# Three weight tiles leave SP's queue for GpSimd's, and zero fills change engine

## The chip, the cores and the metric

One core of a Trainium2 chip runs the whole program. The metric is the device time in microseconds of one execution. Engines are named as in the profile: PE (TensorE), DVE (VectorE), ACT (ScalarE), POOL (GpSimd) and SP (SyncE, which here only issues DMAs).

## The reference

A delta-rule recurrence feeds a gated feed-forward block. For 4 batches and 8 heads, 768 tokens of 48 numbers each:

```python
k_n = k / (np.linalg.norm(k, axis=-1, keepdims=True) + 1e-06)
for t in range(S):
    y[:, :, t] = einsum('bhd,bhde->bhe', q[:, :, t], state)
    v_old = einsum('bhde,bhd->bhe', state, kt)
    state = state + bt * einsum('bhd,bhe->bhde', kt, vt - v_old)
x = y.transpose(0, 2, 1, 3).reshape(B * S, H * D)      # 3072 tokens x 384
xn = x / sqrt(mean(x * x, axis=-1) + 1e-06) * rms_g
g = xn @ w_gate                                        # 384 x 1536
out = (g * sigmoid(g) * (xn @ w_val)) @ w_out          # 1536 x 384
```

q, k, v and beta are float32. The three weight matrices arrive as float64 words, which the kernel takes in as 64-bit integers and turns into float32 itself.

## The kernel before, in words

**Chunks.** The 768 tokens are cut into 6 chunks of 128. In a chunk the recurrence becomes matrix products, if one has the inverse of a triangular matrix for each head. For the first chunk `invert_halves` builds the inverses of 16-blocks on DVE in 15 steps (lines L498 and L505), with all 32 batch-heads on the partitions. The result `ttb` must then be turned so that tokens lie on the partitions: it goes out to DRAM as `td` (L507) and comes back as `tt` (L524); a second matrix, made from it by L510, goes out as `nd` (L516, issued by ACT) and comes back as `ne` (also L524). `halves` then multiplies with `tt` (p_vh, L652; its result is copied out by ACT at L659) and with `ne` (p_wh, L663).

**Order.** For the first 60 units of a hand-made plan nothing is scheduled automatically (`tc.manual_schedule()`): each engine, and each engine's DMA queue, executes in the order in which the Python code emits. `begin` emits the norms of k, the key scores (K phase), the query scores (the loop over `n` after `clear_ttb`, here called the Q phase), and the inversion; then `recur(0, ...)` emits the recurrence of the first chunk, up to its first `yield`. The rest is interleaved by `run_plan`, which takes generators by their times. A DMA issued by SP waits at the head of SP's queue until its semaphore's former user has landed and until its buffer is free; all that is behind it waits too.

**Weights.** They come as 18 tiles of 768 KB, each in two loads of 384 KB, in the order of the list `todo`. `fetch` issues the next tile. Tiles 3 to 6 land in parts of the final weight buffers that are still unused (`spare`), the others in a pool of three (`raw`). The generator `weights` turns a tile into float32 in five DVE steps (L259, L268, L280, L284, L290) after one ACT step (`shrink`, L249, the upper words, buffer `top`); `convert(n)` takes n of these DVE steps. At tile 5 and from tile 7 on, a tile's fourth step also calls `fetch`. A tile index below `AHEAD`, which is 9, goes to SP's queue, the others to POOL's.

**Fills.** `stay_warm(n)` emits n matmuls (two PE instructions each in the trace, L190) whose result nobody reads.

**First norms.** `norm` in the first chunk has ACT square and sum y (L871), POOL add 1e-6 (L879) and raise to the power -0.5 (L880, giving `rs`); `scale` and `transpose_y` then give the input `xt` of the feed-forward block (L894), whose matmuls are L923 and L910, with silu by ACT (L932) and the product h_f by DVE (L934).

Of the kernel before, what the change touches and what calls it, by code (L numbers as in the profile page):

```python
# [18 lines left out]
C = 128  # L19
HC = 64  # L20
# [8 lines left out]
def kernel(  # L29
# [21 lines left out]
    nc = tc.nc  # L51
# [4 lines left out]
    DM = H * D  # L56
# [35 lines left out]
    state = [const.tile([128, NP, 2 * D], FP32, name=f"state{b}") for b in range(B)]  # L92
# [16 lines left out]
    lo, hi = slice(0, HC), slice(HC, C)  # L109
# [28 lines left out]
    def setup():  # L138
        for t in kpad + qpad:
            nc.vector.memset(t[:, :, D:DP], 0.0)  # L140
        nc.scalar.memzero(tt_all)
        for n in range(B):
            load_k(n)
        fetch()

        beta_sb = ttb.rearrange("p k j -> p (k j)")[0:BH, 0:S]
        nc.sync.dma_start(out=beta_sb, in_=beta.rearrange("b h s -> (b h) s"))
        blocks = beta.rearrange("b h (c a i) -> a (b h) c i", a=NBLK, i=W)
        for a in range(NBLK):
            nc.sync.dma_start(out=nbeta[a * BH : (a + 1) * BH], in_=blocks[a])  # L150
        load_q(0)
        fetch()
        load_q(1)
        fetch()
        nc.sync.dma_start(out=g_sb, in_=moe_rms_g.rearrange("(t p) -> p t", p=128))
        nc.vector.memset(half, 0.5)
        nc.vector.memset(mhalf, -0.5)
        make_identity(nc, ident)
        row, col = (
            gblk.bitcast(I32).rearrange("p k j -> p (k j)")[:, C * i : C * (i + 1)] for i in (0, 1)  # L160
        )
        nc.gpsimd.iota(row, pattern=[[0, 128]], base=0, channel_multiplier=1)
        nc.gpsimd.iota(col, pattern=[[1, 128]], base=0, channel_multiplier=0)
        nc.vector.memset(mask[lo, 1], 1.0)
        for i, p in enumerate((lo, hi)):
            nc.vector.tensor_tensor(
                out=mask[p, i], in0=row[p, p], in1=col[p, p], op=ALU.is_lt
            )
        p_fill.append(psum.tile([128, DM], FP32, name="p_fill", tag="out", bufs=2))
# [18 lines left out]
    def stay_warm(n, data=wide):  # L188
        for i in range(n):
            nc.tensor.matmul(  # L190
                p_fill[0].rearrange("p (t m) -> p t m", m=128)[:, 0 : data.shape[1]],
                ident,
                data,
                skip_group_check=True,
            )
# [27 lines left out]
    spare = [wgv_sb[:, t : t + 2, far] for t in range(0, 2 * KT, 2)] + [  # L223
        wo_sb[:, FT // 2 : FT // 2 + 4].rearrange("p (x t) m -> p x (t m)", x=2)
    ]
    AHEAD = 3 + len(spare) + 2

    def fetch():
        i = len(raws)
        if i < len(todo):  # L230
            if 3 <= i < 3 + len(spare):
                raw = spare[i - 3].bitcast(I64)
            else:
                raw = bits.tile([128, 2, WT], I64, name="raw", bufs=3)
            for x, src in enumerate(todo[i][1]):
                (nc.sync if i < AHEAD else nc.gpsimd).dma_start(out=raw[:, x], in_=src)
            raws.append(raw)

    def words(raw):
# [14 lines left out]
    def weights():  # L254
        for i, ((dst, src), raw) in enumerate(zip(todo, raws)):
            low, high = words(raw)
            top = tops[i]
            top_u, dst_u = top.bitcast(U32), dst.bitcast(U32)
            nc.vector.tensor_scalar(  # L259
                out=top_u,  # L260
                in0=top_u,
                scalar1=3,
                scalar2=0x7FFFFFFF,
                op0=ALU.logical_shift_left,
                op1=ALU.bitwise_and,
            )
            yield
            nc.vector.scalar_tensor_tensor(  # L268
                out=top_u,
                in0=high,  # L270
                scalar=0x80000000,
                in1=top_u,
                op0=ALU.bitwise_and,
                op1=ALU.bitwise_or,
            )
            yield
            if i + 1 < len(todo):
                tops.append(shrink(raws[i + 1]))

            nc.vector.tensor_scalar(  # L280
                out=dst_u, in0=top_u, scalar1=0xFF800000, scalar2=None, op0=ALU.bitwise_and
            )
            yield
            nc.vector.scalar_tensor_tensor(  # L284
                out=dst, in0=low, scalar=2.0**-52, in1=dst, op0=ALU.mult, op1=ALU.mult
            )
            if i == 5 or i >= 7:
                fetch()
            yield
            nc.vector.tensor_tensor(out=dst, in0=dst, in1=top, op=ALU.add)  # L290
            yield
        bits_pool.close()
# [3 lines left out]
    def convert(steps):  # L296
        for i in range(steps):
            next(conversion, None)
# [174 lines left out]
    def clear_ttb():  # L473
        nc.gpsimd.memset(ttb, 0.0)  # L474
        nc.gpsimd.memset(ttb.rearrange("p j i -> p (j i)")[:, 0 : W * W : W + 1], 1.0)
# [109 lines left out]
    def recur(c, dt):  # L585
# [196 lines left out]
        if c == 0:  # L782

            halved = [halves(b) for b in units]
            next(halved[0])
            next(halved[1])
            next(halved[0])
            next(halved[1])
            corner(0, None)
            corner(1, None)  # L790
            convert(1)
            corner(None, 0)
            corner(None, 1)
            convert(2)
            inner(0, None, 0)
            inner(1, None, 1)
            stay_warm(1)
            inner(None, 0, None)
            inner(None, 1, None)
            convert(1)  # L800
            u_0, u_1 = us[0], us[1]
            stay_warm(2)
            outer(None, 0)
            outer(None, 1)
            convert(3)
            stay_warm(3)
            transpose_y(0, scale(*ys.pop(0)))
            convert(1)
            stay_warm(2)
            transpose_y(1, scale(*ys.pop(1)))  # L810
            convert(4)
            yield
            update(0, u_0)
            mask_queries(2)
            yield dt
            update(1, u_1)
            reload()
            yield dt
            next(halved[2])
            mask_queries(3)  # L820
            yield dt
            next(halved[3])
            yield dt
            next(halved[2])
            yield dt
            corner(2, None)
            next(halved[3])
            yield dt
            corner(3, 2)
            yield dt  # L830
            inner(None, None, 2)
            corner(None, 3)
            yield dt
            inner(2, None, 3)
            yield dt
            inner(3, 2, None)
            yield dt
            u_2, u_3 = us[2], us[3]
            outer(None, 2)
            yield dt  # L840
            inner(None, 3, None)
            yield dt
            outer(None, 3)
            yield dt
            transpose_y(2, scale(*ys.pop(2)))
            yield dt
            transpose_y(3, scale(*ys.pop(3)))
            yield dt
            update(2, u_2)
            yield dt  # L850
            update(3, u_3)
            reload()
            return
# [117 lines left out]

    def begin():
        setup()
        stay_warm(14, ident[:, None])
        norms = [normalize(n) for n in range(B)]
        for n in (0, 0, 1, 1, 2, 2, 3, 0):
            next(norms[n])
        transpose(0, kpad[0], K0)
        tops.append(shrink(raws[0]))
        for n in (3, 1):  # L980
            next(norms[n])
        transpose(1, kpad[1], K0)
        for n in range(B):
            p_gs = score_part(n, K0)
            if n + 2 < B:
                next(norms[n + 2])
                transpose(n + 2, kpad[n + 2], K0)
            keep_keys(n, p_gs)
            convert((1, 2, 2, 5)[n])
        setup_beta()  # L990
        clear_ttb()
        convert(2)
        for n in range(B):
            transpose(n, qpad[n % 2], Q0)
            stay_warm(2)
            load_q(n + 2)
            fetch()
            load_v(n)
            keep_queries(n, score_part(n, Q0))
            if n in (1, 2):  # L1000
                fetch()
            if n == 0:
                mask_queries(n)
        nc.scalar.memzero(gp_all[HC:C, :, 0:HC])
        invert_halves()
        load_k(B)
        stay_warm(4)
        for t in state:
            nc.scalar.memzero(t)
        stay_warm(6, ttb_all[:, 0:DM].rearrange("p (t m) -> p t m", m=128))  # L1010
        convert(3)
        mask_queries(1)
        convert(3)


    CYC = 3 * FT * B // 2
# [49 lines left out]
```

## Time and profile before

| | |
|---|---|
| median of 10 runs | 873.8 us (872.0 to 879.15) |
| the profiled execution | 873.14 us, span 871.4 us |
| PE busy | 826.3 us, 95% of the span |
| DVE busy | 403.0 us, 46% |
| ACT busy | 257.1 us, 30% |
| POOL busy | 98.4 us, 11% |
| DVE busy in 80 to 100 us | 18.84 of 20 us |
| PE's granted clock, 48 to 70 us | 0.50 |

The span is the profiled execution's; about 1.7 us of its time lie around it. Times in a row of the timeline or the chain are counted from the span's start. A row of the timeline has start, duration (first start to last end where rows are merged), engine and line, operation, output <- inputs, form and count. "SPq" and "ACTq" are the queues that issue DMAs; the duration there is that of issuing, and the time to landing is told in the list of DMA issues.

### The profile page before, as it was taken

The page shows a single profiled execution, that of the slowest core. Times are in us where ns is not written, and L with a number is a line of the kernel's source. Part 1 is how long each engine was busy: PE and PEld are TensorE (multiplying, and loading weights), DVE is VectorE, ACT ScalarE, POOL GpSimd, SP SyncE. Part 2 cuts the span into 40 slices and gives each one's busy share as a digit, 9 for nine tenths or more (in the row PEclk, how much of TensorE's full clock was granted, in tenths as well). Part 3 has the DMA queues.
Part 4 walks back from the last instruction along what each step waited for, and adds up shares of the span by engine and source line. Part 5 has one row for each costly group of instructions (what it writes and reads, how often), then busy time and mean ns, then how long its engine had stood idle before and what let it go on. Part 6 is the DMA issues. An engine that isn't in the chain of part 4 may idle for free.

```text
span 871.4 us, 20949 instructions
## 1 busy us (share of the span) xinstructions
PE 826.3 (95%) x8990; PEld 636.7 (73%) x8990; DVE 403.0 (46%) x1014; ACT 257.1 (30%) x663; POOL 98.4 (11%) x130
## 2 busy tenths in 40 slices
PE   7839979798999999999999999999999999999998
PEld 6437767576887777787777787777787777777776
DVE  6826976994343671333671333581333581220100
ACT  5423545312334212334112334112334212220111
POOL 3001244200140000230000140000130000000000
PEclk8958998999999999999999999999999999999999
DMA  7961444303222122122122122122121112000000
GB/s 184 264 170 40 110 128 102 111 1 99 52 66 37 31 76 38 39 65 37 31 76 38 39 65 37 31 72 41 39 51 22 32 70 35 3 19 1 19 0 19
DMA packets 153405, 52.16 MB, mean 60 GB/s; under 512 B 144448, under 2 KB 147520, under 8 KB 153312
## 3 DMA queue, kind: packets, MB, share of 16 engines
q1 hardware_dynamic: 125744, 40.06, 18.6%
q0 software_dynamic: 1440, 7.08, 2.4%
q10 hardware_dynamic: 26128, 3.68, 2.4%
q8 instruction: 71, 1.16, 0.5%
q14 instruction: 22, 0.18, 0.1%
HBM read 36.64 MB, written 14.16 MB: 58 GB/s over the span
## 4 chain that ended last, share of the span: by engine, by line
PE 79%; DVE 13%; issue 2%; ACT 2%; DMA 2%; POOL 1%; SPq 0%; ACTq 0%; DVEq 0%
PE p_gv L923 38%; PE p_o L910 18%; DVE tmp L537 4%; DVE ttb L546 3%; PE p_g L353 3%; PE p_y L688 3%; PE p_z L744 2%; PE p_t L337 2%; PE p_k L726 2%; PE p_y L726 2%; PE p_v L602 2%; PE p_x L762 1%; PE p_z L753 1%; PE p_w L609 1%; DVE h_f L934 1%
## 5 line engine op out<-in xcount | busy, mean ns | idle before, releaser
L923 PE MATMUL p_gv<-xt,wgv_sb 128*128 128x256 f32 x1728 | 413.0, 385 | 0.6 <-DVE xt L894 0.6
L923 PEld LDWEIGHTS p_gv<-xt,wgv_sb 128*128 128x128 f32 x1728 | 320.3, 190 | 63.8 <-issue 3.1
L910 PE MATMUL p_o<-wo_sb,h_f 128*128 128x384 f32 x576 | 215.4, 498 | 11.3 <-DVE h_f L934 11.3
L934 DVE TENSOR_TENSOR h_f<-sil,p_gv 128x256 f32<-128x256 f32 x144 | 60.2, 418 | 242.1 <-ACT sil L932 242.0
L932 ACT ACTIVATE sil<-p_gv 128x256 f32<-128x256 f32 x144 | 55.3, 384 | 333.4 <-PE p_gv L923 316.6
L910 PEld LDWEIGHTS p_o<-wo_sb,h_f 128*128 128x128 f32 x576 | 104.4, 191 | 63.6 <-DVE h_f L934 17.0
L537 DVE SCALAR_TENSOR_TENSOR tmp<-gblk,nbeta,ttb 128x31 f32<-128x31 f32 (+15 forms) x155 | 62.2, 401 | 4.6
L367 DVE TENSOR_TENSOR gp<-p_g,mask 64x128 f32<-64x128 f32 (+1 forms) x160 | 38.0, 277 | 40.0 <-ACT gp L363 35.4
L546 DVE TENSOR_TENSOR ttb<-ttb,tmp 128x31 f32<-128x31 f32 (+15 forms) x155 | 53.0, 342 | 4.9
L317 POOL TENSOR_TENSOR knrm<-ksum,half 128x8 f32<-128x8 f32 x24 | 41.8, 1745 | 66.1 <-DVE ksum L316 66.1
L879 POOL TENSOR_SCALAR ms<-ms 128x1 f32<-128x1 f32 x24 | 6.2, 257 | 322.5 <-ACT y L871 322.0
L342 ACT COPY kqt<-p_t 128x512 f32<-128x512 f32 x48 | 28.1, 585 | 32.4 <-PE p_t L337 31.7
L474 POOL MEMSET ttb<- 128x1024 f32 x6 | 5.7, 955 | 241.5 <-DMA td<-ttb 232.0
L353 PE MATMUL p_g<-kqt 64*64 64x192 f32 x640 | 31.8, 331 | 1.1 <-ACT gp L363 0.9
L744 PEld LDWEIGHTS p_z<-v_raw,tt 64*64 64x64 f32 x768 | 25.8, 142 | 9.2 <-issue 7.2
L622 ACT COPY vs<-p_v 32x256 f32<-32x256 f32 x48 | 17.4, 363 | 44.6 <-PE p_w L609 22.1
L353 PEld LDWEIGHTS p_g<-kqt 64*64 64x64 f32 x640 | 23.3, 132 | 8.4 <-issue 5.3
L762 PE MATMUL p_x<-tt,gp 64*64 64x64 f32 x384 | 28.8, 229 | 0.1
L744 PE MATMUL p_z<-v_raw,tt 64*64 64x48 f32 x768 | 28.8, 227 | 0.0
L362 ACT COPY gp<-p_g 128x128 f32<-128x128 f32 x80 | 21.3, 266 | 20.4 <-PE p_g L353 19.0
L753 PE MATMUL p_z<-u,x 64*64 64x48 f32 x384 | 27.1, 220 | 0.0
L762 PEld LDWEIGHTS p_x<-tt,gp 64*64 64x64 f32 x384 | 25.6, 142 | 1.9 <-issue 1.3
(110 smaller groups left out, 782.7 us busy)
## 6 DMA issues: line engine op xcount, KB each, us to landing
kpad<-in_k_dram SPq DMA_DIRECT2D x24, 192.0 KB, 2.7
qpad<-in_q_dram SPq DMA_DIRECT2D x24, 192.0 KB, 2.6
v_raw<-in_v_dram SPq DMA_DIRECT2D x24, 192.0 KB, 3.0
out_dram<-o_sb SPq DMA_DIRECT2D x24, 192.0 KB, 1.9
gblk<-gd SPq DMA_DIRECT2D x6, 512.0 KB, 3.2
td<-ttb SPq DMA_DIRECT2D x6, 512.0 KB, 2.6
gd<-gp ACTq DMA_DIRECT2D x80, 32.0 KB, 1.7
nd<-gblk SPq DMA_DIRECT2D x5, 512.0 KB, 2.7
```

What stands on the lines that cost most here:

```text
L317: nc.gpsimd.tensor_tensor(out=knrm, in0=ksum, in1=half, op=ALU.pow)
L353: nc.tensor.matmul(to, pair[d, K1 if i else K0], pair[d, places], skip_group_check=True)
L367: nc.vector.tensor_tensor(out=to[p, :, place], in0=p_g[p, :, place], in1=mask[p, i, None].to_broadcast([p.stop, 2, HC]), op=ALU.mult,)
L537: nc.vector.scalar_tensor_tensor(out=tmp, in0=gblk[:, i, None, i + 1 :].to_broadcast(shape), scalar=nbeta[:, c, i : i + 1], in1=ttb[:, 0 : ...
L546: nc.vector.tensor_tensor(out=to, in0=to, in1=tmp, op=ALU.add)
L744: nc.tensor.matmul(p_zs[b_z][p, h], tt[b_z][p, h], r[p, h], start=(h == 0), stop=(p is lo), skip_group_check=True,)
L753: nc.tensor.matmul(p_zs[b_u][hi, h], x2s[b_u][:, h], us[b_u][lo, h], start=False, stop=True, skip_group_check=True,)
L762: nc.tensor.matmul(p_x[lo, h], gp[b_x][hi, h, HC * K0 : HC * (K0 + 1)], tt[b_x][hi, h], skip_group_check=True,)
L910: nc.tensor.matmul(p_o[i], h_f[:, i * C : (i + 1) * C], wo_sb[:, f], start=(f == f0), stop=(f == f1 - 1),)
L923: nc.tensor.matmul(p_gv[:, i], wgv_sb[:, i * KT + t, f * 128 : (f + 1) * 128], xt[:, t], start=(t == 0), stop=(t == KT - 1),)
L932: nc.scalar.activation(out=sil, in_=p_gv[:, 0], func=ACTF.Silu)
L934: nc.vector.tensor_tensor(out=h_f, in0=sil, in1=p_gv[:, 1], op=ALU.mult)
```

## The change

In the Q phase, SP keeps one weight tile in each of the first three passes (tiles 3, 4 and 5). Tiles 6, 7 and 8 are issued on POOL's queue, right after `outer(None, 1)` of the first recurrence, so behind the two first norms' POOL instructions. `fetch` gets the issuing function as an argument in place of the comparison with `AHEAD`. The loads of v for n = 2 and 3 move behind `invert_halves`. The zero fills of the four `state` tiles and of the part of `gp` move from ACT to POOL, to a place ahead of the Q phase. The ACT step for tile 3 (`shrink(raws[3])`) is emitted ahead of `invert_halves`, and `weights` skips it later. Fills: two more behind the inversion, one fewer at each of two places in the recurrence. One conversion step fewer is taken at the end of `begin`. In the changed file, line numbers from `fetch` on are smaller by 1 up to `recur`'s first chunk.

```diff
-        fetch()
+        fetch(nc.sync.dma_start)          # three times, in setup
...
-    AHEAD = 3 + len(spare) + 2
-
-    def fetch():
+
+    def fetch(dma):
         i = len(raws)
...
-                (nc.sync if i < AHEAD else nc.gpsimd).dma_start(out=raw[:, x], in_=src)
+                dma(out=raw[:, x], in_=src)
...
-            if i + 1 < len(todo):
+            if len(tops) == i + 1 < len(todo):
                 tops.append(shrink(raws[i + 1]))
...
             if i == 5 or i >= 7:
-                fetch()
+                fetch(nc.gpsimd.dma_start)
...
             inner(1, None, 1)
-            stay_warm(1)
             inner(None, 0, None)
             inner(None, 1, None)
             convert(1)
             u_0, u_1 = us[0], us[1]
-            stay_warm(2)
+            stay_warm(1)
             outer(None, 0)
             outer(None, 1)
+            for i in range(3):
+                fetch(nc.gpsimd.dma_start)
             convert(3)
...
         clear_ttb()
+        for t in state:
+            nc.gpsimd.memset(t, 0.0)
+        nc.gpsimd.memset(gp_all[hi, :, 0:HC], 0.0)
         convert(2)
         for n in range(B):
             transpose(n, qpad[n % 2], Q0)
             stay_warm(2)
             load_q(n + 2)
-            fetch()
-            load_v(n)
+            if n < 3:
+                fetch(nc.sync.dma_start)
+            if n < 2:
+                load_v(n)
             keep_queries(n, score_part(n, Q0))
-            if n in (1, 2):
-                fetch()
             if n == 0:
                 mask_queries(n)
-        nc.scalar.memzero(gp_all[HC:C, :, 0:HC])
+        tops.append(shrink(raws[3]))
         invert_halves()
+        for n in (2, 3):
+            load_v(n)
         load_k(B)
         stay_warm(4)
-        for t in state:
-            nc.scalar.memzero(t)
-        stay_warm(6, ttb_all[:, 0:DM].rearrange("p (t m) -> p t m", m=128))
+        stay_warm(8, ttb_all[:, 0:DM].rearrange("p (t m) -> p t m", m=128))
         convert(3)
         mask_queries(1)
-        convert(3)
+        convert(2)
```

More of the change, by code (lines that the diff above doesn't have):

```diff
@@ L151, in setup @@
         load_q(0)
-        fetch()
+        fetch(nc.sync.dma_start)
         load_q(1)
-        fetch()
+        fetch(nc.sync.dma_start)
         nc.sync.dma_start(out=g_sb, in_=moe_rms_g.rearrange("(t p) -> p t", p=128))
@@ L996, in begin @@
             load_q(n + 2)
-            fetch()
-            load_v(n)
+            if n < 3:
+                fetch(nc.sync.dma_start)
+            if n < 2:
+                load_v(n)
             keep_queries(n, score_part(n, Q0))
-            if n in (1, 2):
-                fetch()
             if n == 0:
                 mask_queries(n)
-        nc.scalar.memzero(gp_all[HC:C, :, 0:HC])
+        tops.append(shrink(raws[3]))
         invert_halves()
+        for n in (2, 3):
+            load_v(n)
         load_k(B)
         stay_warm(4)
-        for t in state:
-            nc.scalar.memzero(t)
-        stay_warm(6, ttb_all[:, 0:DM].rearrange("p (t m) -> p t m", m=128))
+        stay_warm(8, ttb_all[:, 0:DM].rearrange("p (t m) -> p t m", m=128))
         convert(3)
         mask_queries(1)
-        convert(3)
+        convert(2)
     CYC = 3 * FT * B // 2
```

## The prediction

> **What bounds the kernel now.** I read the page's 40 slices first. They show a hole near the start that averages hide: TensorE is busy for 95% of the span, but its third slice reads 7 and its clock there 5.
>
> ```profile
> PE   7839979798999999999999999999999999999998
> PEclk8958998999999999999999999999999999999999
> ```
>
> A slice is 21.8 us, so the hole is somewhere in 43.6 to 65.4. After slice 11 TensorE is at 9 in every slice: time won before that passes to the end if what follows is fed as before. Next, the chain of waits, limited to the first 150 us, shows what fills the hole (start, duration, what):
>
> ```profile
> 41.54 6.34 DMA nd<-gblk
> 47.89 0.38 SPq L131
> 48.38 3.58 DMA td<-ttb
> 51.98 2.19 DMA tt<-td
> 54.17 0.18 issue
> 54.35 1.76 ACT state L1009 x4
> 56.11 1.28 ACT top L249 x2
> 57.39 0.19 issue
> 57.58 0.26 ACT vs L659
> 57.89 1.78 PE p_wh L663 x115
> ...
> 71.00 0.89 PE p_fill L190 x2
> 71.89 1.99 PE p_z L753 x32
> 73.88 1.49 PE p_fill L190 x4
> ```
>
> The inverse of the 16-blocks is done when L505 ends at 39.47 (VectorE starts L510 at 39.50). It must go to DRAM (td) and come back turned (tt), but td is issued only at 48.38. The order of SP's queue and the queue's own waits say why:
>
> ```profile
> 37.80 2.43 SPq L236 DMA_DIRECT2D raw<-in_moe_w_val_dram  x2
> 40.33 0.38 SPq L123 DMA_DIRECT2D qpad<-in_q_dram  x1
> 40.81 2.17 SPq L236 DMA_DIRECT2D raw<-in_moe_w_out_dram  x2
> 47.89 0.38 SPq L131 DMA_DIRECT2D v_raw<-in_v_dram  x1
> 48.38 0.52 SPq L507 DMA_DIRECT2D td<-ttb  x1
> ```
>
> ```profile
> SPq L131 <- DMA nd<-gblk: 4.9, 1, 4.9
> ```
>
> The last v_raw load stands ahead of td in program order and waits until nd has landed; nd takes 6.34 us because weight tiles 7 and 8 (numbered from 0) are in flight, at 360 to 420 GB/s in the windows from 40 to 48. So td is 8.9 us late for no reason of data.
>
> **What the Trainium skill says.** "TensorE: Matmul & The Clock Gate", Part 1: the array's clock is halved after an idle window of about 3.4 us and restored after a busy one. The trace agrees: the last fill ends at 43.75, the granted clock is 1.00 in 46:47, 0.58 in 47:48, 0.50 from 48, and returns in 71:72, after dense matmuls from 67.3. "Trainium Kernel Development and Optimization", Key Constraints: DMAs from SP, ScalarE and GpSimd run on the same 16 engines, so changing the issuer frees no bandwidth, only order; the 6.34 us of nd fits that. "SBUF — State Buffer", SBUF: two separate sides: VectorE in its two-port modes and GpSimd exclude each other, and descriptors of GpSimd's DMAs can starve, with a figure of 620 ns grown to 3100 ns. The trace shows the lock (L259 took 0.92 us beside the 0.95 us memset L474 at 21.2, 0.55 us alone) but no starving: GpSimd's pair of loads at 79.79 took 1.40 us to issue, those at 96.3, under a full VectorE, 0.55 us each.
>
> **The change, part by part.**
>
> *Tiles 6, 7, 8 leave SP; v_raw 2 and 3 go behind the inversion.* Ahead of td, SP loses six loads of 384 KB and two of 192 KB. Ahead of it remains the load of qpad for n=3, which waits for transposes done by 34.8. So td issues when ttb is complete: 39.5. Landing: 2.6 us is the median of six td, 3.58 the one here; I take 2.8, giving 42.3. The first tt pair then needs 3.25 us as before (51.97 to 55.2): 45.5. nd is issued at 41.54 as before (VectorE's L510 sets it) but lands in 2.7 (median) to 6.34 us; without weights in flight I take 3.0: 44.6. The ne pair follows with 0.5 us for the second issue and 3.2 us to land (median here): 48.2. L652 takes 2.06 us from 45.5, then L659: 47.9. p_wh thus starts at 48.3, held now by ne instead of td, against 57.89: **9.6 us**, with ends of 8.0 (both transfers slow) and 10.5. The tt loads of batches 2 and 3 are queued behind ne on SP and land by about 50; their users come 30 us later.
>
> *Zero fills to GpSimd.* ScalarE loses L1004 (1.91 us, in its own idle time) and four of L1009 (1.76 us), which stood between the tt issue and L659. That is already in the 47.9. GpSimd gains four fills of 384 columns and one of 2048: from 0.95 us per 1024 columns, 0.36 each and 1.9, an estimate of 3.3 us from 22.6 on, in its idle 54.5 us. They can block VectorE up to 26; VectorE has 0.86 us of idle before L485, which waits for gblk until 29.90. Cost between 0 and 1.0; I take 0. No gain below nothing, since that start is a DMA's.
>
> *Upper words of tile 3 early.* L249 (0.88 us) moves from 56.0 into ScalarE's idle time at 38.3, and VectorE can do L259 and L268 near 45.5 instead of 56.9. They were beside TensorE's L652 then: 0 on the path, but L669's copies find VectorE free.
>
> *Fills on TensorE.* Two more behind the inversion: 12 instructions in 4.03 us become 16, ending at 45.1 instead of 43.75, just before L652: 0 (at most 0.3). One fewer ahead of L753 and one fewer ahead of L688: 0.89 and half of 1.49, both on the chain, and their data (ScalarE's x and VectorE's u) are 0.3 us or less from ready: **1.6 us**, at worst 0.9.
>
> *One conversion step fewer before the recurrence.* A step of 0.55 to 0.96 us moves into the stretch from 82, where VectorE is 94% busy (18.84 of 20 us in 80:100): a cost of 0.4, between 0 and 1.
>
> *Tiles 6 to 8 loaded by GpSimd behind the first norms.* Six issues of about 0.65 us follow the second rs (79.76 before). A GpSimd tile issued at 79.79 had landed by 84.0, so tile 6 lands at rs + 4.2 to 5. ScalarE needs 0.93 us for its upper words, VectorE wants them at rs + 5.8 (L259 at 85.58), and half a step later now: covered, barely. Tile 7 lands near rs + 6.5 to 7, and ScalarE takes it at rs + 6.7 (86.45), ahead of the first silu: 0.4 us, between 0 and 3 with ScalarE's queue behind it. Tile 8 near rs + 9, wanted at rs + 11.5. Tile 9 issues behind six loads, wanted at rs + 21. The norm's own pow is ahead of the loads; the next, in prepare, is 24 us later.
>
> Sum: 9.6 + 1.6 - 0.4 - 0.4 = 10.4 us off the profiled execution, 873.14 (span 871.4 and 1.7 around it), 862.7. The median of the ten runs stands 0.66 above that execution: **863.3**.
>
> **The rivals.**
> 1. *Warm clock.* With fills to 45.1 and no idle window, the clock may stay at 1.00 through the narrow matmuls until 71. For: the hole is gone. Against: busy shares near half in small pieces; the clock fell again near 129 after 3.4 us of which about 1.4 were busy. Gain: p_z and p_x from 67.4 to 71.0 cost 3.6 us at half clock, about 2.2 at full, and the pieces from 57.9 to 66.4 perhaps 1.3 less: 2.7 us more, 860.6. The main forecast has the clock fall within this stretch anyway, as before.
> 2. *Late tiles.* Tile 6 and 7 land 2 to 4 us later than I take, because four tiles (3.1 MB) leave together at 300 to 400 GB/s: in-order ScalarE then holds silu and VectorE stands. Also the shorter fills may put the return of the clock one window later. 3 us less gain: 866.3.
> 3. *Starved descriptors, slower.* In the stretch 70 to 90 VectorE alternates conversions and masks; should each of the six issues take 3.1 us, the skill's figure, instead of 0.65, tile 8 is 14.7 us late, less the 2.5 it has in hand: ScalarE and VectorE wait 12.2 us in order, 863.3 + 12.2 = 875.5. It turns the gain into a loss from 2.8 us per issue on (6 x 2.15 - 2.5 = 10.4), by over 0.3% from 3.3. Against: the 0.55 us issues under a full VectorE.
> 4. *The change doesn't do what it says:* another owner holds td in SP's queue (the qpad load, if tile 5 is still landing at 40). Then about 873, no change.
>
> **How the numbers follow.** Main forecast 0.50, warm clock 0.26, late tiles 0.13, starved 0.07, no change 0.04. Main and warm reach 858; late tiles reach 868. Range 857.5 to 868.5 leaves out the last two cases and the tails. Of the starved case I count 0.06 as slower, 0.01 as same. 0.3% is 2.6 us, about what a measurement of this kernel can tell from no change: faster 0.89, same 0.05, slower 0.06.
>
> **What would show it.** Right: td<-ttb issued at 39.5 to 40.5, nd landing in about 3 us, p_wh at 48 to 49.5, rs near 69, L259 of tile 6 without a wait on ScalarE over 1 us, and from 200 us on the same rows shifted by about 10 us. Wrong: an SP wait ahead of td; ScalarE idle before L248 on a GpSimd load for over 2 us; GpSimd issues over 1 us; or a clock row of 9 and more in the third slice, which is the second case.

## The result, and the profile after

The changed kernel takes 866.7 us (median of 14 runs, 863.7 to 874.4) against 873.0 for the kernel before (51 runs). The ratio is 0.9921, interval 0.9904 to 0.9938: faster by about 6.9 us (6.3 by the two medians). The forecast was 863.3 and a gain of 10.4 us; the range of 857.5 to 868.5 holds the result.

The profiled execution of the changed kernel (863.31 us, span 861.5) is one of its fastest, so its total flatters the change. First the page's slices of this kernel:

```profile
PE   7879979789999999999999999999999999999998
PEclk9969989999999999999999999999999999999999
```

The third slice of PE now reads 7, where the line of the kernel before has 3; the clock in it is still only 6 (5 before). Next, the chain of waits of the changed kernel (start, duration, what). "issue" in it is time in which the engine waited for nothing that the profile shows; here such pauses fall between the narrow matmuls of the recurrence, those of 32 by 32:

```profile
39.19 3.70 DMA nd<-gblk
43.31 3.07 DMA ne<-nd
46.42 1.74 PE p_wh L662 x109
48.16 1.62 issue
...
52.70 1.43 issue
...
62.35 0.84 PE p_fill L190 x2
63.19 2.02 PE p_y L687 x64
```

And the timeline of the same kernel, with the issuing queues:

```profile
34.24 0.38 SPq L123 DMA_DIRECT2D qpad<-in_q_dram  x1
...
37.22 0.33 SPq L506 DMA_DIRECT2D td<-ttb  x1
...
39.19 0.35 ACTq L515 DMA_DIRECT2D nd<-gblk  x1
...
41.71 0.90 SPq L523 DMA_DIRECT2D tt<-td  x2
```

td goes out 0.03 us after ttb is complete (37.19) instead of 8.9 us later; nd needs 3.7 us instead of 6.3, and ne is the last to arrive ahead of p_wh, as the prediction had it. td itself took longer to land than before, 4.4 us instead of 3.6. What follows divides the executions at the same four places: ttb complete (start of L509, L510 before), start of p_wh, end of the second rs, and the issue of the second chunk's td. The two further profiles of the unaltered changed kernel come from the experiments. The last stretch includes the 1.7 us that lie outside the span.

| us | before | after | after, 2nd | after, 3rd |
|---|---|---|---|---|
| start to ttb | 39.50 | 37.19 | 38.39 | 39.25 |
| ttb to p_wh | 18.39 | 8.94 | 9.28 | 10.19 |
| p_wh to second rs | 21.87 | 21.40 | 21.39 | 21.95 |
| second rs to second td | 121.84 | 124.18 | 124.40 | 125.78 |
| second td to the end | 671.54 | 671.60 | 671.06 | 672.11 |
| sum without the start | 833.64 | 826.12 | 826.13 | 830.03 |

The first row is code that the change barely touches, and it varies by 2 us between executions of one kernel; 2.3 us of the 9.8 between the two profiled executions lie there. The other rows leave 7.5, 7.5 and 3.6 us, 6.2 on average, in line with the timed 6.9. In the third execution the granted clock fell to half three times between the norms and the second td (at 122, 166 and 194 us), in the kernel before and in the other two only once. About 9 us were won between ttb and p_wh; 2.3 to 3.9 us were given back between the norms and the second td.

### The profile page after: what moved, and what is told of

Read it like the earlier page. It is cut to its first block, busy times and chain, and to the rows that moved or that the text cites. A ratio compares the mean times of both kernels' runs of the same rounds, so it can differ in the third digit from the quotient of the medians.

```text
span 861.5 us, 20958 instructions
## 1 busy us (share of the span) xinstructions
PE 824.3 (96%) x8990; PEld 634.5 (74%) x8990; DVE 404.8 (47%) x1014; ACT 253.2 (29%) x658; POOL 104.2 (12%) x141
## 4 chain that ended last, share of the span: by engine, by line
PE 78%; DVE 13%; issue 3%; DMA 3%; ACT 2%; POOL 1%; SPq 1%; ACTq 0%; DVEq 0%; POOLq 0%
PE p_gv L923 38%; PE p_o L910 18%; DVE tmp L536 4%; DVE ttb L545 4%; PE p_g L352 3%; PE p_y L687 3%; PE p_z L743 2%; PE p_t L336 2%; PE p_k L725 2%; PE p_y L725 2%; PE p_v L601 2%; PE p_x L761 1%; PE p_z L752 1%; DVE h_f L934 1%; PE p_w L608 1%
```

## The experiments

All ratios are to the kernel before, on the same chip, with 95% intervals.

**The changed kernel again.** No edit.

> The changed kernel, unaltered, for a second profile: the first one started 2.3 us earlier than the kernel before (ttb complete at 37.2 against 39.5), in code that the change doesn't touch. If that is the phase of the clock's window, this profile's ttb lies elsewhere between 36.5 and 40 and its time moves with it (863 to 868), while ttb to p_wh stays at 9.0 to 9.6 us (18.4 before). If the change itself brings the earlier start, ttb is complete at 37.0 to 37.5 again.

865.9 us, ratio 0.992 (0.9889 to 0.9951). ttb is complete at 38.39 and p_wh follows 9.28 us later. So the early start of the first profile belongs to that execution, and the gain behind ttb to the change. In these executions the granted clock falls and returns in different places of the first 30 us (half clock from 19.4 to 22.8 in the first profile, from 11.1 to 14.5 and from 24.8 to 28.2 in the second).

**Order alone.** The kernel before, with two loads moved.

```diff
-            load_v(n)                 # Q phase
+            if n < 2:
+                load_v(n)
...
         invert_halves()
+        for n in (2, 3):
+            load_v(n)
         load_k(B)
```

> The kernel before with one edit: the loads of v for n = 2 and 3 move behind the inversion; tiles 6 to 8 stay in SP's queue ahead of td. Theory of the queue: td issues when SP has issued tile 8, near 43 instead of 48.4, still beside weights: ttb to p_wh falls from 18.4 to about 13 us, and the gain is 4 to 5 us (868 to 869). Rival, that bandwidth and not order holds td and nd: both still take 5 to 6 us to land, ttb to p_wh stays over 16 us and the gain is under 2 us.

871.6 us, ratio 0.9973 (0.9958 to 0.9988). The timeline of SP's queue in this kernel:

```profile
38.68 1.96 SPq L236 DMA_DIRECT2D raw<-in_moe_w_out_dram  x2
40.74 0.42 SPq L507 DMA_DIRECT2D td<-ttb  x1
48.43 0.86 SPq L524 DMA_DIRECT2D tt<-td  x2
```

td is issued 3.3 us after ttb (37.43) instead of 8.9, but takes 7.6 us to land, with two weight tiles in flight; ttb to p_wh is 17.5 us. The rival holds: moving the v loads alone is worth 0.9 us of that wait. The time fell by 2.4 us (1.0 to 3.7), a little more than the rival's 2.

**Tiles alone.** The changed kernel, with the v loads where they were.

```diff
-            if n < 2:
-                load_v(n)
+            load_v(n)
...
-        for n in (2, 3):
-            load_v(n)
```

> The changed kernel with the loads of v for n = 2 and 3 back in the Q phase, ahead of td in SP's queue; tiles 6 to 8 stay on GpSimd. With the run that moved v alone (ttb to p_wh still 17.5 us), this is the other half. If the traffic of the tiles is what counted, td issues within 1 us of ttb and ttb to p_wh is 9 to 10.5 us, time within 1 us of the changed kernel. If both edits are needed, td waits again behind v_raw and ttb to p_wh is over 12 us.

866.2 us, ratio 0.992 (0.9905 to 0.9935), the same as the change. SP's queue in this kernel:

```profile
36.99 2.30 SPq L131 DMA_DIRECT2D v_raw<-in_v_dram  x1
39.40 0.64 SPq L506 DMA_DIRECT2D td<-ttb  x1
44.20 0.93 SPq L523 DMA_DIRECT2D tt<-td  x2
```

ttb was complete at 38.81, so td is 0.6 us late, and p_wh comes 10.6 us after ttb, 0.4 to 1.6 us later than in the three profiles of the change. Both v loads may stand ahead of td at that cost; what counts is that the three weight tiles are gone. With them go two things at once: their traffic, and their own places ahead of td in SP's queue. Compared with the run that moved the v loads alone, td is issued 2.7 us sooner after ttb (0.6 against 3.3) and lands 2.9 us faster (4.7 against 7.6). No run keeps the traffic there and changes the queue, so the two are not separated further.

**Tiles early on SP.** The three tiles are issued behind the ne loads.

```diff
         load_k(B)
+        for i in range(3):
+            fetch(nc.sync.dma_start)
         stay_warm(4)
...
-            for i in range(3):
-                fetch(nc.gpsimd.dma_start)
```

> The changed kernel with tiles 6 to 8 issued on SP right behind the ne loads and the late v and k loads, near 50 us, instead of on GpSimd behind the norms. Theory of late tiles (they cost 1.3 us between rs and 26 us after it, and the 4.1 us wait of ScalarE for tile 6): that wait is gone, the second rs to p_x L761 falls from 26.3 to about 25 us, time 1 to 1.5 us less than the changed kernel. Theory of the conversion step: no difference in that stretch. Rival: the tiles' traffic at 50 to 58 holds back the instruction fetch, the gaps of TensorE there grow and 1 us or more is lost.

873.1 us, ratio 0.9977 (0.9956 to 0.9997): nearly the whole gain is gone, far more than the rival asked. It is not gone in every execution: the 22 runs spread from 866.3 to 876.4 us; the six fastest (up to 870.3) have a mean granted clock of 0.978 to 0.980, the others 0.968 to 0.976. In the profiled execution (873.06 us) ttb to p_wh is 9.2 us, but p_wh to the second rs takes 25.7 us (21.4). The chain of waits of this kernel shows one gap more than that of the changed kernel, inside p_z:

```profile
54.71 1.70 issue
...
61.04 1.62 issue
```

The windows of this kernel, then of the changed one (stretch, length, busy us of PE, PEld, DVE, ACT and POOL with their instructions, granted clock, DMA share, GB/s):

```profile
60.00:64.00 4.00, 2.38 (x66) 2.22 (x63) 1.13 (x2) 0.59 (x1) 0.00 (x0) 0.50 0.67 258
64.00:68.00 4.00, 4.00 (x54) 3.91 (x52) 1.21 (x3) 0.59 (x1) 0.00 (x0) 0.50 0.02 4
68.00:72.00 4.00, 4.00 (x66) 2.92 (x66) 3.50 (x5) 0.58 (x2) 0.00 (x0) 0.62 0.02 4
```

```profile
56.00:60.00 4.00, 4.00 (x121) 3.94 (x123) 2.78 (x4) 1.76 (x5) 0.00 (x0) 0.50 0.01 4
60.00:64.00 4.00, 4.00 (x79) 3.29 (x77) 2.66 (x5) 0.59 (x1) 0.00 (x0) 0.95 0.00 0
```

With the tiles on the DMA engines at 258 GB/s, PE pauses for 1.6 us at the start of its first dense stretch, and the clock returns at 71.0 instead of 60.4. Counted from the start of p_wh, that is some 8 us more at half clock, for p_z, p_y and the fills. That the pause comes from the tiles' traffic is an inference from the one falling on the other, and the pause does not explain all: from 64 to 68 PE is busy throughout and the clock stays at 0.50, whereas in the changed kernel it had returned after 4 such microseconds. The second rs to the second td was 126.9 us, but in it the clock fell to half four times, so this stretch says nothing on what earlier tiles bring there.

**Tiles early on ScalarE's queue**, after the narrow matmuls.

```diff
             inner(None, 1, None)
+            for i in range(3):
+                fetch(nc.scalar.dma_start)
             convert(1)
...
-            for i in range(3):
-                fetch(nc.gpsimd.dma_start)
```

> The changed kernel with tiles 6 to 8 issued on ScalarE's queue behind L778, six issues of about 0.5 us near 61 us, six us ahead of GpSimd's place[...]. Theory of late tiles: ScalarE no longer waits for tile 6 (4.1 us) and 7 (1.1 us), the second rs to the second td falls from 124.2 to about 123. Theory of the step: it stays at 124.2. If the issues last longer than 3 us, y L871 is late and p_z to rs grows past 8 us.

867.0 us, ratio 0.9924 (0.9901 to 0.9948): no faster than the change. ScalarE's 4.1 us wait for tile 6 is gone; the second rs to the second td is 123.4 us, 0.8 to 1.0 less than in the first two profiles of the change. But the run "Tiles alone", with the tiles on GpSimd and the same wait of 4.1 us, has 123.5 us there as well. So the lateness of the tiles was visible, and that it costs time is not shown.

**The conversion step put back**, in two runs, and a third with the tiles on ScalarE's queue.

```diff
         mask_queries(1)
-        convert(2)
+        convert(3)
```

> The changed kernel with the conversion step that was dropped put back (convert(3) ahead of the recurrence). Theory of the step: VectorE is the bound from rs to the second td (124.2 us after the change, 121.8 before), so this stretch falls by 1 to 2.4 us and the time by as much. Rival, late tiles: the stretch stays within 0.5 us of 124.2.

> Both: tiles 6 to 8 on ScalarE's queue behind L778, and the conversion step put back. If the two losses behind the norms add up (step 1.4 us, tiles about 1), the second rs to the second td is 121.5 to 122.5 us, near the 121.8 of before, and the time is 2 to 3 us less than the changed kernel: 863 to 864. If they are one loss seen twice, it stays at 123.

> The changed kernel unaltered, as the measure for the three runs beside it: 865.5 to 867; second rs to second td 124.2 to 124.4 us.

> The changed kernel with the conversion step put back, a second time, since its first comparison (863.9 against 865.9) had overlapping intervals. Theory of the step: 863 to 865, and the second rs to the second td 122.5 to 123.2. If the first was chance, 865.5 to 867 and 124 or more.

| run | us | beside it, without the step | second rs to second td |
|---|---|---|---|
| step back | 863.9 (0.9862 to 0.9915) | 865.9 | 122.98 |
| step back, tiles on ScalarE | 864.0 (0.9876 to 0.9911) | 867.0 (tiles on ScalarE) | 122.51 |
| step back, again | 865.1 (0.9884 to 0.9933) | 867.5 (ratio 0.9936, 0.9916 to 0.9957) | 122.40 |

Each pair's intervals overlap, but all three say 2.0 to 3.0 us, and the stretch is 0.9 to 3.4 us shorter. (The unaltered kernel itself missed what was expected of it: 867.5 us instead of 865.5 to 867, and 125.8 us in the stretch instead of 124.2 to 124.4.) The windows of VectorE alone over this stretch (second rs to second td, cut where the second gblk is loaded) say why. Before, after, and with the step back again:

```profile
79.76:167.70 87.94, 70.70 (x141) 0.96 0.42 115
167.70:201.60 33.90, 31.81 (x80) 1.00 0.05 17
```

```profile
67.53:155.00 87.47, 69.88 (x133) 0.96 0.49 143
155.00:191.70 36.70, 34.65 (x90) 1.00 0.04 16
```

```profile
71.00:159.40 88.40, 70.54 (x141) 0.96 0.50 141
159.40:193.40 34.00, 31.91 (x81) 1.00 0.06 17
```

VectorE's work in the stretch is 102.5 us before, 104.5 after and 102.5 with the step back; its idle time is 19.3, 19.6 and 20.0. The work hardly varies between executions: 104.5 to 104.9 us in the eight profiles of the change and its variants without the step, 102.4 to 102.6 in the three with it. The idle time is 18.9 to 20.5 us where the clock fell once or twice in the stretch, and 21.1 to 22.8 in the four profiles where it fell three or four times. So two more microseconds of work are two microseconds of time, and of the 3.4 us of the third pair about one belongs to the clock, which fell three times in the one profile and once in the other.

**Fills put back.**

```diff
             inner(1, None, 1)
+            stay_warm(1)
             inner(None, 0, None)
...
-            stay_warm(1)
+            stay_warm(2)
             outer(None, 0)
```

> The changed kernel with the two removed fills of the recurrence put back (stay_warm(1) ahead of L752, stay_warm(2) ahead of L687). The prediction priced them at 1.6 us on the chain; between p_wh and the second rs the change saved only 0.5 us (21.87 to 21.40). If the price was right and the longer waits for instructions (3.0 us in 46 to 55 after, 2.0 before) ate it, this stretch grows to 22.9 to 23.2 us here and the time by 1.5 us. If fills there are all but free, it stays within 0.5 us of 21.4.

869.5 us, ratio 0.9941 (0.9922 to 0.9959). p_wh to the second rs is 22.8 us against 21.4, 21.4 and 22.0 in the three profiles of the change. A part of this stretch is PE's pauses ("issue"), which vary from one execution to the next. Without the two pauses of each chain the stretch is 19.8 us in the kernel before, 19.8 with the fills back, and 18.4, 18.2 and 17.3 in the three profiles of the change. So the two fills cost 1.4 us or more. The time is 1.7 us more than the change's by the ratios, whose intervals overlap; behind the norms this execution took 127.6 us, and in it the clock fell to half four times, first at 94.5 to 97.9. Why it fell there stays open.

**Zero fills back on ScalarE.**

```diff
-        for t in state:
-            nc.gpsimd.memset(t, 0.0)
-        nc.gpsimd.memset(gp_all[hi, :, 0:HC], 0.0)
...
+        nc.scalar.memzero(gp_all[HC:C, :, 0:HC])
         tops.append(shrink(raws[3]))
...
+        for t in state:
+            nc.scalar.memzero(t)
         stay_warm(8, ...)
```

> The changed kernel with the zero fills back on ScalarE (L1004 behind the query copies, four of 0.5 us ahead of L658). The prediction priced their move at 0 since p_wh waits for ne: ttb to p_wh stays at 9.0 to 9.7 us, time within 1 us of the changed kernel. Rival: the four fills hold L658 as they did before, ttb to p_wh grows by 1 to 1.7 us and the time with it.

866.3 us, ratio 0.9925 (0.9899 to 0.9951), beside 867.5 for the unaltered change on the same chip; ttb to p_wh is 9.7 us (10.2 there). The move of the zero fills is worth nothing that can be measured, as priced.

**More steps ahead.** Tiles on ScalarE's queue as above, and

```diff
-        convert(2)
+        convert(5)
```

> Tiles 6 to 8 on ScalarE's queue behind L778, and three more conversion steps ahead of the recurrence than the change has (convert(5)), in VectorE's idle 3 us ahead of L669 and 4 us behind it. Theory of the step: each step moved out of the stretch behind the norms is worth up to its 0.6 to 1.0 us there, so second rs to second td is 120.5 to 122 us and the time 861 to 863.5. Rival: VectorE is no longer the bound once the step of before is back; then 122.5 us and 864 as with one step.

863.7 us, ratio 0.9902 (0.987 to 0.9934). VectorE alone over the same stretch:

```profile
69.08:156.10 87.02, 71.85 (x142) 0.98 0.44 119
156.10:188.90 32.80, 29.26 (x77) 1.00 0.05 17
```

101.1 us of work in 119.8: 1.5 us less work, and a stretch 2.7 us shorter, than with one step and the tiles on the same queue. The rest goes with the clock, which was at half for 3.4 us in this stretch and for 13.7 in the other. This profiled execution, 860.43, is the shortest of all; over its runs the median is not apart from the one-step versions. With either number of steps the median is below both the kernel before and the change, at about 864 to 865.

## Why the prediction was right, and where it was off

**The wait removed: right in size, partly wrong in cause.** 9.6 us were forecast between ttb and p_wh; the three profiles show 9.5, 9.1 and 8.2. ne was last, as worked out, in the first two; in the third PE also paused for 2.6 us ahead of p_wh, for no reason that the profile shows. That the size fits so well is in part luck: td took 4.4 us to land where 2.8 were taken, and nd 3.7 instead of 3.0, while the p_vh matmuls, at full clock until 46.7, took 1.5 us instead of 2.06. The prediction named both the queue and the traffic, but its sentence that td was 8.9 us late "for no reason of data", behind a v_raw load, put order first. The two half edits show that the place of the v loads alone gains 0.9 us of this wait, and taking the tiles away alone about 7.8. The 6.34 us of nd in the profile before was the better sign. Two readings were off without harm to the sum: the third slice of PE in the kernel before is 3, not 7 (that is the first), and the traffic from 40 to 48 us was 307 to 419 GB/s in windows of 1 us, not 360 to 420.

**The fills: the price was right, the balance was not.** 1.6 us were forecast, and putting them back fits that, but p_wh to the second rs became only 0.5 us shorter in the first two profiles and no shorter in the third. In the chains, PE's pauses among the narrow matmuls after the start of p_wh are 1.62 and 1.43 us after, 1.24 and 0.80 before: 1.0 us was lost there, 1.2 and 2.6 in the two further profiles. I had no term for these pauses. Why they are longer stays open; that PE waits for its instructions there, as some of the expectations have it, is not shown.

**The dropped conversion step: this is the term that was mis-sized.** It was priced at 0.4 us, one operation of 0.55 to 0.96 at half weight, with 1.0 as the upper end. It cost 2.0 to 3.0 us of time, and 2.0 us of VectorE's work in the traces. VectorE is busy for 84% of the stretch behind the norms, but the length of the stretch follows its work, so the step counts in full (0.96, L289). The other 1.1 us are operations that took longer in the shifted order. The longest of them, in the timeline of the changed kernel, is an L258, which takes 0.55 us alone, beside a memset of GpSimd:

```profile
148.92 1.93 DVE L258 TENSOR_SCALAR top<-top 128x768 uint32<-128x768 uint32 x1
149.46 0.97 POOL L473 MEMSET ttb<- 128x1024 f32 x1
```

Such collisions are in the kernel before as well (an L268 of 0.96 took 1.92 at 151.3); after the change they cost more.

**The tiles on GpSimd: landed roughly as worked out.** The six issues took 0.55 to 0.77 us. Tile 6 landed 4.6 us after the second rs (4.2 to 5 forecast), tile 7 at 7.7 (6.5 to 7). ScalarE waited, in the waits of the changed kernel:

```profile
ACT top L248 <- DMA wo_sb<-in_moe_w_val_dram: 4.1, 1, 4.1
```

That broke my own sign of under 1 us for ScalarE. silu came at rs + 10.0 against 8.9 before, but the stretch was 123.4 us without this wait and 123.5 in a variant with it, so that it costs time is not shown.

**The rivals.** Warm clock: no, the clock is 0.50 from 46.7 to 60.4; the narrow matmuls from 44.7 to 48.2 didn't hold it, although PE's busy time there has few gaps. Late tiles: present, but not shown to cost anything. The result of 866.7 lies beside this rival's 866.3 all the same; that is a coincidence of numbers, since most of what is missing from the gain is the dropped step and PE's pauses. Starved descriptors: no issue was over 0.8 us. (The prediction gives the 3100 ns for a whole DMA; the rival lent them to a single issue.) The change doing nothing: no.

**The sum.** 9.6 + 1.6 - 0.4 - 0.4 = 10.4 became 8.9 + 0.3 - 2.9 - 0.1 = 6.2, as means of the three profiles; the third term is the stretch from the norms to the second td, the last what lies behind it.

## What to carry to other kernels

Ask of a late transfer both what stands ahead of it in its queue and what shares the engines with it: here the small loads ahead of it were worth 0.9 us alone, and the weight tiles, which did both, 7.8. In a stretch whose length follows the work of one engine, an operation moved into it costs its full length and what it collides with, so fill that engine's idle time ahead of the stretch first. Look also at what PE is doing when background transfers run: behind the norms, beside dense matmuls at full clock, the three tiles cost nothing that could be shown; in the one kernel that ran them where PE started a dense stretch at half clock, most of the gain was lost in most executions.

## What had not been expected of the hardware

In the first chunk of the changed kernel and its variants, td's 512 KB landed in 2.6 to 4.9 us, with at most the last 1.1 us of a weight load beside it; beside two weight tiles, in the run that moved only the v loads, it took 7.6 us. PE paused for 0.8 to 2.9 us at a time between narrow matmuls in every profile, and once for 1.6 us inside p_z when 2.3 MB of tiles were landing; in that profile the clock was at half for 23.9 us on end, in the changed kernel for 13.7. The changes of the granted clock in a profile lie whole multiples of 3.41 us apart (in the kernel before: at 9.62, 16.44, 47.16, 71.06, 129.08 and 135.91 us), so the clock changes what a pause costs in steps. An execution's first 39 us vary by 2 us between runs of one kernel, so single profiles should be compared by stretches, not by their ends, and with the falls of the clock in each stretch beside them.
